# A two-layer decode kernel: one q weight block kept from its first read, a place made of small buffers, and K loads one head further ahead

## The chip, the cores and the metric

The kernel runs on one core of a Trainium2 chip. A core has a matrix engine (PE, whose weight loads are shown apart as PEld), a vector engine (DVE), a scalar engine (ACT), a general one (POOL) and a sync engine (SP) that here does nothing but issue transfers from HBM; 16 DMA engines carry them. Each engine runs its own instructions in order, and engines wait for each other through semaphores. The metric is the device time of one execution in microseconds (us).

## What is computed

Four residual blocks: attention with a cached window, a gated feed-forward block (GLU), and the same two again with the same weights and the same caches.

```python
x = x + attn(layernorm(x));  x = x + glu(layernorm(x))
x = x + attn(layernorm(x));  x = x + glu(layernorm(x))

def attn(x):                          # x: [4, 1, 512], 32 query heads, 8 KV heads of 128
    q = (x @ wq).reshape(4, 1, 32, 128).transpose(0, 2, 1, 3)
    k, v = k_cache[:, :, -2048:], v_cache[:, :, -2048:]     # each repeated for 4 query heads
    p = softmax(q @ k.T * 128 ** -0.5)
    return (p @ v).transpose(0, 2, 1, 3).reshape(4, 1, 4096) @ wo

def glu(x):                           # 512 -> 1792 -> 512
    return (sigmoid(x @ w_gate) * (x @ w_up)) @ w_down
```

The batch is 4. K and V of one KV head and all four batches are 2 MB each in bf16, the q and output weights 4 MB each, the three GLU weights 1.8 MB each.

## The kernel before

**Memory.** `arena` has 50 slots of 128 x 2048 bf16 (512 KB). Two neighbouring slots are a tile (1 MB). 32 slots hold K of all eight heads: K is read once, and the second layer uses it again. The other 18 slots are nine tiles that a pool hands out in turn: for q weights, output weights (four tiles, kept for the second layer), V, and the GLU weights. A tile goes back to the pool when its last user has been recorded; `done` counts users, `fill` takes the next load from the list when the pool, or a named place, has room. Beside the arena lie some 25 small buffers, among them `prow` (the probabilities of one head), `ebuf` (probabilities after transposition, in two halves, one for even and one for odd heads), `qbd` and `qh` (q as the score matmuls need it) and `mxt`.

**Half places.** At the change of layers, weights come in blocks of half a tile. Each block has a home in `homes`: a half of a tile that an earlier load left. Tile names are those of their first occupants: `Y` and `Z` (the two V blocks of head 7), `GA` (the first V block of head 6) and `GB` (a tile taken for nothing but its two halves, after the first layer's loads). A home is written as a pair, such as `(GB, 1)` for the second half. V of head 7 must stay for the second layer; parts of it are stashed in PSUM by transposes on DVE (L578, L600) and brought back (L593, L606), which frees halves of `Y` and `Z`.

**Order of transfers.** SP issues the list in order (L398), each transfer waiting for its place alone: q weights (4 tiles), K of heads 0 and 1, then per head h: K of head h + 2, the output weights of two heads (for h = 0, 2 and 4), V of head h in two blocks. Then the last output weights (a block and two halves), gate and up weights (4 blocks of 448 KB each), down weights (3 blocks of 4 columns of 512 and one of 2), the q weights again in eight blocks of 512 KB, V of heads 6 to 0 as far as it was not kept, and the GLU weights again. A load that waits for its place holds all behind it.

**Order of compute.** Every operation is recorded with what it reads and writes; a list scheduler with estimated durations and due times fixes each engine's order at build time, and semaphore waits are derived from it. For one head of the first layer: four DVE transposes of K (L854), a mask (L872) and the scores (L883) on PE, the maximum on DVE (L896 to L908), the exponential on ACT (L911), a permutation on PE, ACT and DVE (L924 to L931), 32 matmuls with V (L973) for each of the two V blocks, normalisation on DVE (L981, L996) and the output weights (L1162). The second layer's q comes in two halves of four blocks each (`q_mms`, L795): the half `i = 1` first, which serves heads 7 to 4, then `i = 0`. In the second layer two places that last held q blocks become work buffers (`wide_buffers`); each head's scores free two K tiles, which V then uses.

Of the kernel before, what the change touches and what calls it, by code (L numbers as in the profile page):

```python
# [6 lines left out]
F32 = mybir.dt.float32  # L7
BF16 = mybir.dt.bfloat16
# [270 lines left out]
def build(nc, A_x, A_k, A_v, A_wq, A_wo, B_wg, B_wu, B_wd, out, cfg=None):  # L279
# [28 lines left out]
    FCC = 2 * SLOT // D  # L308

# [12 lines left out]
    with es:  # L322
# [9 lines left out]
        ones_f = sb("ones_f", [128, 32], F32)  # L332
        perm = sb("perm", [128, 128], BF16)
        sel_f = sb("sel_f", [128, NR], F32)
        sel_b = sb("sel_b", [128, NR], BF16)
        s3 = sb("s3", [128, 2 * 3], BF16)
        sres = sb("sres", [128, 2], F32)
        sel_r = sb("sel_r", [128, 2 * REP], F32)
        maskr = sb("maskr", [128, 32], F32)
        mxt = sb("mxt", [128, 2 * 32], F32)  # L340
        nmax = sb("nmax", [128, 6], F32)
        msk_s = sb("msk_s", [128, 32], BF16)
        msk_m = sb("msk_m", [128, 2], BF16)
        psm = sb("psm", [128, 2], F32)
# [4 lines left out]
        maskp = sb("maskp", [128, REP], F32)  # L349
        msks = sb("msks", [128, 22], F32)  # L350
# [4 lines left out]
        lnr = sb("lnr", [128, 2 * NB], F32)  # L355
        lnd = sb("lnd", [128, NB], F32)
        lnv = sb("lnv", [128, NB], F32)
        inv_d = sb("inv_d", [128, 1], F32)
# [4 lines left out]
        ident = ebuf[:, 0:64].bitcast(BF16)  # L363
        ps = es.enter_context(nc.psum_tensor("ps", [128, 8, 512], F32))
# [14 lines left out]

        def slot_ap(s):  # L380
            return arena[:, s * SLOT:(s + 1) * SLOT]

# [39 lines left out]
        GB = ("pair",)  # L422
        base = {}
# [10 lines left out]
        def take_load():  # L434
            take_k()
            assert can_take()
            name, emit = loads.pop(0)
            if name in homes:
                hfree.difference_update(home(name))
                s = home(name)[0]  # L440
            else:
                s = pool.alloc()
            where[name] = s
            if name in (Y, Z, GA, GB):
                base[name] = s
            if name == GB:
                hfree.update((s, s + 1))
            emit(s)
# [38 lines left out]
        def load_half(name, src, rate, size, where_):  # L487
            left[name] = 1
            homes[name] = [where_]
            on_free[name] = lambda s: hfree.add(s)  # L490

            def emit(s):
                dma(str(name), slot_ap(s)[:, 0:size], src, w=[("slot", s)], rate=rate)
            loads.append((name, emit))
# [59 lines left out]
        def load_glu(k):  # L554
            for nm, src in (("wg", wg_d), ("wu", wu_d)):
                if k == 0:
                    for c in range(NC):
                        load_half((nm, c, k), src[:, c, :], "bw_3k", F,
                                  (((GB, 0), (GB, 1), (GA, 0), (Y, 0)), ((Y, 1), (Z, 0), (GB, 0), (GB, 1)))[nm == "wu"][c])
                    continue  # L560
                for cc in range(NC // 2):
                    load((nm, cc, k), 2, "bw_3k", (2 * F, src[:, 2 * cc:2 * cc + 2, :], False))
            for (a, b) in bounds_of(k):
# [45 lines left out]
        def load_v(h, bp, k, n_use):  # L609
            name = ("V", h, bp, k)  # L610
            tiles = {(HKV - 2, 0): ((Y, 0),), (HKV - 3, 1): ((Y, 1), (GB, 0))}.get((h, bp)) if k else None
            if tiles is not None:
                halves[h, bp] = []
                for n, tile in enumerate(tiles):
                    half = ("Vh", n, h, bp, k)
                    load_half(half, pair_d(A_v, h, bp)[:, :, n * SLOT:(n + 1) * SLOT], "bw_4k", SLOT, tile)
                    halves[h, bp].append((half, 0))
                if len(tiles) == 1:
                    halves[h, bp].append((KEPT, 0))
                return  # L620
            load(name, n_use, "bw_8k", (2 * SLOT, pair_d(A_v, h, bp), True))
# [9 lines left out]

        P.op("gpsimd", "ones", 200.0, lambda g: g.memset(ones_f[:], 1.0), w=[("ones_f",)])
        P.op("gpsimd", "ident_b", 300.0,
# [9 lines left out]
        for jh in range(2):  # L643
            for bp in range(2):
                for i in range(2):
                    z0 = 16 * jh + 8 * bp + REP * i
                    P.op("gpsimd", "perm%d_%d_%d" % (jh, bp, i), 200.0,
                         lambda g, jh=jh, bp=bp, i=i, z0=z0: g.affine_select(
                             perm[:, :].rearrange("p (a z) -> p a z", a=4)[:, :, z0:z0 + REP],
                             ones_f[:, 0:NR].rearrange("p (a r) -> p a r", a=4),  # L650
                             [[-REP, 4], [-1, REP]], ALU.is_equal, 0.0,
                             base=-(64 * jh + 32 * bp + 16 * i), channel_multiplier=1),
                         r=[("ones_f",), ("perm",)], w=[("perm", jh, bp, i)])
# [5 lines left out]
             r=[("ones_f",)], w=[("msk_s",)])  # L659
# [4 lines left out]
             r=[("ones_f",)], w=[("msk_m",)])  # L664
        P.op("vector", "sel_f", 200.0,
             lambda v: v.tensor_reduce(sel_f[:, :], perm[:, :].rearrange("p (g x) -> p x g", x=NR), AXX, ALU.add),
             r=perms, w=[("sel_f",)])
        P.op("gpsimd", "sel_b", 200.0, lambda g: g.tensor_copy(sel_b[:, :], sel_f[:, :]),
             r=[("sel_f",)], w=[("sel_b",)])
        P.op("vector", "sel_r", 100.0,  # L670
             lambda v: v.tensor_reduce(sel_r[:, :], sel_f[:, :].rearrange("p (g y) -> p y g", g=2), AXX, ALU.add),
             r=[("sel_f",)], w=[("sel_r",)])
# [111 lines left out]
        def q_mms(k, i, qb, cs):  # L784
            for c in cs:
                name, o = wq_part(k, c, i)
                s = need(name)

                src = slot_ap(s) if k else tile_ap(s)
                rd = tok(s)[:1] if k else tok(s)  # L790

                def e_q(pe, c=c, src=src, o=o):
                    last = None
                    for hh in range(4):
                        last = pe.matmul(ps[32 * hh:32 * hh + NB, qb, :], xn[:, c * NB:(c + 1) * NB],  # L795
                                         src[:, o + hh * 512:o + (hh + 1) * 512],
                                         start=(c == 0), stop=(c == NC - 1))
# [373 lines left out]
        def attn_first():  # L1171
# [8 lines left out]
            for h in range(HKV):  # L1180
# [124 lines left out]
        def glu(k, b0, b1, add=None, last=False):  # L1305
# [6 lines left out]
            NH = NFC * nb  # L1312
            NF = F // 4
            half = D // 2

            def x_rows():
# [3 lines left out]
                     lambda g: g.affine_select(idf, ones_f[:, 0:1].broadcast_to([128, 128]), [[1, 128]], ALU.is_equal, 0.0,  # L1320
                                               base=0, channel_multiplier=-1),
                     r=[("ones_f",)], w=[("prow",)])
# [11 lines left out]
            for n, nm in enumerate(("wg", "wu")):  # L1334
                for c in range(NC):
# [3 lines left out]
                    def e_g(pe, c=c, s=s, n=n):  # L1339
                        last = None  # L1340
                        for g in range(4):
# [4 lines left out]
                         r=[("slot", s), ("xn",)], w=[("gu", n)], banks=(gub[n],))  # L1346
# [8 lines left out]
                if n == 0:  # L1355
                    P.op("vector", "gs%d" % k, c_dve(NH),
                         lambda v: v.tensor_tensor(egv, tv, lnr[:, 0:nb].unsqueeze(1).broadcast_to([128, NFC, nb]), ALU.mult),
                         r=[("e", 0), ("e", 1), ("lnr", 0)], w=[("eg",), ("q", 0)])
# [11 lines left out]
                 r=[("e", 0), ("e", 1), ("eg",), ("q", 0)], w=[("hT",)])  # L1370
            if last:
                x_rows()
                for (a, b) in bounds_of(k):
# [3 lines left out]
                    def e_d(pe, a=a, b=b, s=s):  # L1377
                        last_ = None
                        src = tile_ap(s)
                        for fc in range(a, b):  # L1380
# [7 lines left out]
                         r=tok(s) + [("hT",)], w=[("orow",)], banks=(PBS[0],))  # L1388
# [10 lines left out]
            for (a, b) in bounds_of(k):  # L1399
# [3 lines left out]
                def e_d(pe, a=a, b=b, s=s):  # L1403
                    last = None
                    src = slot_ap(s)
                    for fc in range(a, b):
# [7 lines left out]
                     r=tok(s)[:1] + [("hT",)], w=[("cb",)], banks=(CB,))  # L1414
# [24 lines left out]
        loads.append((GB, lambda s: None))  # L1439
# [97 lines left out]
```

## Time and profile before

| | |
|---|---|
| Median of 3 runs | 178.61 us (178.56 to 178.66) |
| Span of the profiled execution, first to last instruction | 177.0 us |
| PE / DVE / ACT / POOL busy | 102.3 / 104.6 / 32.7 / 21.6 us |
| Share of the chain of waits: DMA / DVE / PE | 38% / 32% / 18% |
| HBM read | 70.26 MB |
| Time from issue to landing, V blocks / second q blocks (median) | 22.4 / 6.2 us |

The profile is of one execution. In the views, a line such as L398 is that of the kernel's source, `x8` counts instructions or transfers, and an arrow `out<-in` names what is written and read. In the chain of waits each row gives a start, a length and what was at work; a DMA row runs from its issue to its landing. In a window row, each engine's busy time stands with its instruction count in brackets; then come the granted PE clock, the DMA engines' busy share and their rate.

SP's timeline shows the queue: K and V are issued far ahead, and at the change of layers each block a few microseconds ahead.

```profile
62.12 24.83 SPq L398 DMA_DIRECT2D arena<-in_A_v_cache_dram  x6
95.72 1.30 SPq L398 DMA_DIRECT2D arena<-in_A_wo_dram  x3
97.06 4.95 SPq L398 DMA_DIRECT2D arena<-in_B_w_gate_dram  x4
...
113.03 9.84 SPq L398 DMA_DIRECT2D arena<-in_A_wq_dram  x8
123.83 17.84 SPq L398 DMA_DIRECT2D arena<-in_A_v_cache_dram  x14
```

The columns are start, length from the first to the last of the group's issues, queue, line, transfer and count.

### The profile page before, as it was taken

How to read it: one execution, taken by the hardware profiler on the slowest of the kernel's cores; microseconds unless marked ns; L12 is line 12 of the kernel's file. 1: busy time of each engine (PE TensorE's matmuls, PEld its weight loads, DVE VectorE, ACT ScalarE, POOL GpSimd, SP SyncE). 2: the span in 40 equal slices, each digit the busy share in tenths (PEclk: the TensorE clock that was granted, in tenths of full speed). 3: DMA queues.
4: the chain of work that ended last, by engine and by line, in shares of the span. 5: the costliest groups of instructions: out<-in, count | busy, mean ns of one | idle time of the engine just before them, and what ended most of it. 6: DMA issues, size and time to landing. Idle time of an engine off the chain costs nothing.

```text
span 177.0 us, 3893 instructions
## 1 busy us (share of the span) xinstructions
PE 102.3 (58%) x1641; PEld 55.0 (31%) x1653; DVE 104.6 (59%) x256; ACT 32.7 (18%) x87; POOL 21.6 (12%) x88
## 2 busy tenths in 40 slices
PE   0536236382842634607418866456886999776663
PEld 0203112241431431603404852052323444435322
DVE  7307997838477375594383772304299999742351
ACT  2002031312030210300301101000043365430011
POOL 6100010101010100100100100000011454342000
PEclk9999999999999999999999999999999999975555
DMA  6999999999999999999999999999999999999980
GB/s 179 418 429 428 420 422 416 416 420 426 411 414 429 415 422 418 415 420 426 411 420 428 400 403 403 409 401 387 404 429 409 420 418 422 413 417 405 413 351 28
DMA packets 12882, 70.52 MB, mean 398 GB/s; under 512 B 1336, under 2 KB 1344, under 8 KB 6720
## 3 DMA queue, kind: packets, MB, share of 16 engines
q1 hardware_dynamic: 12856, 70.26, 97.4%
q8 instruction: 13, 0.21, 0.5%
q14 instruction: 5, 0.04, 0.1%
q10 hardware_dynamic: 8, 0.00, 0.0%
HBM read 70.26 MB, written 0.00 MB: 397 GB/s over the span
## 4 chain that ended last, share of the span: by engine, by line
DMA 38%; DVE 32%; PE 18%; issue 4%; SPq 4%; ACT 2%; DVEq 0%; ACTq 0%
DMA arena<-in_B_w_down_dram 15%; DMA arena<-in_A_v_cache_dram 15%; DVE arena L854 11%; PE ps L883 7%; DVE nmax L896 5%; DMA arena<-in_B_w_gate_dram 4%; DMA arena<-in_A_wq_dram 4%; SPq L398 4%; PE ps L973 3%; PE ps L872 2%; DVE nmax L900 2%; DVE mxt L904 2%; DVE ebuf L931 2%; PE ps L1162 2%; DVE arena L1064 2%
## 5 line engine op out<-in xcount | busy, mean ns | idle before, releaser
L854 DVE STREAM_TRANSPOSE arena<-arena 128x1024 f32<-128x1024 f32 x32 | 37.0, 1202 | 0.0
L883 PE MATMUL ps<-arena,qbd 128*32 128x512 bf16 x256 | 25.6, 537 | 0.0
L896 DVE TENSOR_REDUCE nmax<-ps 128x1 f32<-128x512 f32 x16 | 10.8, 675 | 19.4 <-PE ps L883 19.3
L973 PE MATMUL ps<-ebuf,arena 128*128 128x8 bf16 x576 | 17.7, 168 | 7.5 <-DMA arena<-in_A_v_cache_dram 4.4
L872 PE MATMUL ps<-msk_m,msk_s 128*32 128x512 bf16 x64 | 8.6, 526 | 23.1 <-DVE arena L854 21.8
L973 PEld LDWEIGHTS ps<-ebuf,arena 128*128 128x128 bf16 x576 | 16.8, 104 | 9.5 <-DMA arena<-in_A_v_cache_dram 5.5
L911 ACT ACTIVATE prow<-ps,nmax 128x512 bf16<-128x512 f32 x16 | 11.0, 687 | 35.1 <-DVE nmax L908 29.5
L847 ACT CAST qbd<-ps 128x256 bf16<-128x256 f32 x16 | 5.9, 370 | 45.0 <-PE ps L883 35.1
L940 POOL CAST s<-psm 128x1 bf16<-128x1 f32 x9 | 1.7, 187 | 84.0 <-ACT prow L911 84.0
L883 PEld LDWEIGHTS ps<-arena,qbd 128*32 128x32 bf16 x256 | 8.4, 121 | 10.4 <-issue 7.7
L795 PE MATMUL ps<-arena,xn 128*4 128x512 bf16 x64 | 8.5, 572 | 4.9 <-DMA arena<-in_A_wq_dram 4.4
L926 ACT CAST prow<-ps 128x512 bf16<-128x512 f32 x16 | 9.4, 585 | 9.9 <-PE ps L973 2.1
L1342 PE MATMUL ps<-arena,xn 128*4 128x448 bf16 x64 | 7.7, 547 | 4.2 <-DMA arena<-in_B_w_up_dram 1.9
L931 DVE STREAM_TRANSPOSE ebuf<-prow 128x256 f32<-128x256 f32 x16 | 7.0, 435 | 3.8 <-ACT prow L926 3.7
L872 PEld LDWEIGHTS ps<-msk_m,msk_s 128*32 128x32 bf16 x64 | 1.7, 98 | 24.1 <-DVE arena L854 22.7
L773 ACT ACTIVATE lnv<-ps 128x4 f32<-128x4 f32 x4 | 0.7, 173 | 41.0 <-PE ps L769 41.0
L1055 PE MATMUL ps<-arena,ebuf 128*32 128x512 bf16 x112 | 7.9, 405 | 0.2 <-DVE nmax L908 0.2
L842 PE MATMUL ps<-qh,eyew 32*128 32x64 bf16 x64 | 5.6, 217 | 3.7 <-ACT qbd L847 2.4
L807 DVE STREAM_TRANSPOSE ebuf<-ps 128x512 f32<-128x512 f32 x3 | 2.1, 717 | 9.4 <-PE ps L795 9.3
L1351 DVE STREAM_TRANSPOSE ebuf<-ps 128x448 f32<-128x448 f32 x4 | 2.6, 650 | 7.1 <-PE ps L1342 7.1
L1162 PE MATMUL ps<-onp,arena 128*128 128x16 bf16 x144 | 5.3, 175 | 2.5 <-DVE onp L996 2.2
L981 DVE TENSOR_TENSOR onb<-ps,rinv 128x16 bf16<-128x16 f32 x9 | 1.7, 185 | 8.3 <-PE ps L973 8.1
(112 smaller groups left out, 132.2 us busy)
## 6 DMA issues: line engine op xcount, KB each, us to landing
arena<-in_A_v_cache_dram SPq DMA_DIRECT2D x27, 1024.0 KB, 22.4
arena<-in_A_k_cache_dram SPq DMA_DIRECT2D x16, 1024.0 KB, 25.1
arena<-in_A_wq_dram SPq DMA_DIRECT2D x4, 1024.0 KB, 8.0
arena<-in_A_wq_dram SPq DMA_DIRECT2D x8, 512.0 KB, 6.2
arena<-in_A_wo_dram SPq DMA_DIRECT2D x3, 1024.0 KB, 26.2
arena<-in_B_w_down_dram SPq DMA_DIRECT2D x4, 512.0 KB, 6.4
arena<-in_B_w_gate_dram SPq DMA_DIRECT2D x4, 448.0 KB, 8.3
arena<-in_B_w_up_dram SPq DMA_DIRECT2D x4, 448.0 KB, 6.2
```

The lines of the kernel that those rows point to most:

```text
L795: last = pe.matmul(ps[32 * hh:32 * hh + NB, qb, :], xn[:, c * NB:(c + 1) * NB], src[:, o + hh * 512:o + (hh + 1) * 512], start=(c == 0), s ...
L854: P.op("vector", "T%d_%d" % (h, t), c_dve(1024), lambda v, v32=v32: v.transpose(v32, v32), r=[("slot", 4 * h + t)], w=[("slot", 4 * h + t)])
L872: last = pe.matmul(ps[32 * gi:32 * gi + 32, bank, :], msk_s[:, :], msk_m[:, :].unsqueeze(1).broadcast_to([128, 256, 2]), start=True, stop= ...
L883: last = pe.matmul(ps[32 * gi:32 * gi + 32, bank, :], qbd[:, q0:q0 + 32], kt[:, cp // 2, cp % 2, jh * NJ:(jh + 1) * NJ, :], start=False, s ...
L896: lambda v: v.tensor_reduce(nmax[:, k2:k2 + 1], ps[:, bank, :], AXX, ALU.max),
L911: lambda a: a.activation(prow[:, :].rearrange("p (m x t) -> p m x t", x=32, t=2), ps[:, bank, :].rearrange("p (m t x) -> p m x t", x=32, t ...
L926: P.op("scalar", "pc" + tag, c_act(512), lambda a: a.copy(prow[:, :], ps[:, pb, :]), r=[("ppb", pb)], w=[("prow",)], banks=(pb,))
L931: P.op("vector", "pt" + tag, c_dve(256), lambda v: v.transpose(et, prow[:, :].bitcast(F32)), r=[("prow",)], w=[("e", k2)])
L973: last = pe.matmul(ps[:, ob, bp * 8:bp * 8 + 8], src[:, j * 128:(j + 1) * 128], ev[:, j % 2, j % 16 // 2, x0:x0 + 8], start=(j == 0), stop ...
L1055: last = pe.matmul(ps[32 * g:32 * g + 32, ob, :], ew[:, g, mq, t], src.rearrange("p (m t d) -> p t m d", t=2, d=128)[:, t], start=(n == 0) ...
L1162: last = pe.matmul(ps[:, WB, c * NR:(c + 1) * NR], tile_ap(s)[:, o + r_ * D + c * 128:o + r_ * D + (c + 1) * 128], ov[:, r_ * NR:(r_ + 1) ...
L1342: last = pe.matmul(ps[32 * g:32 * g + NB, gub[n], 0:NF], xn[:, c * NB:(c + 1) * NB], slot_ap(s)[:, g * NF:(g + 1) * NF], start=(c == 0), s ...
```

## The change

It has four parts.

1. `WQ` names the tile of the first q weight block, `("wq", 0, 0)`. It is no longer given back after the first layer's q: its second half keeps the data, which is the second layer's block `("wq", 0, 1, 1)` (`keep_wq`), and its first half becomes a half place. The second layer's q weights are seven transfers in place of eight.
2. The pair `GB` is gone. Eight tiles rotate in the first layer in place of nine.
3. `prow`, `qbd`, `qh`, `mxt` and `ebuf` become parts of one buffer `side`; its first 2048 columns are a slot of their own, `SP`, used between the layers for a gate block, a down block and a q block. A transfer into it carries the tokens of all buffers in it (`stok`), and it is given free at the first layer's head 6. The other small buffers are packed into `small`; `hT` moves onto `rinv`, the GLU's `eg` from `qbd` to `onp`, and the constant of ones onto `ebuf`, with one extra memset for `one`. The down blocks become 3, 4, 4 and 3 columns.
4. `AHEAD = 3`: K of heads 0 to 2 come before the first V, and K of head h + 3 before V of head h.

```diff
+    AHEAD = 3
...
-        prow = sb("prow", [128, 512], BF16)
-        ebuf = sb("ebuf", [128, 512], F32)
-        qbd = sb("qbd", [128, 2 * NB * 4 * NR], BF16)
-        qh = sb("qh", [128, 2 * 64], BF16)
+        side = sb("side", [128, 1536 + 1024], BF16)
+        prow, qbd, qh = side[:, 0:512], side[:, 512:512 + 2 * NB * 4 * NR], side[:, 1024:1024 + 2 * 64]
+        mxt = side[:, 1152:1152 + 4 * 32].bitcast(F32)
+        ebuf = side[:, 1536:1536 + 1024].bitcast(F32)
+        small = sb("small", [128, 60], F32)
...
-        hT = sb("hT", [128, NFC * NB], BF16)
+        hT = rinv[:, 0:NFC * NB // 2].bitcast(BF16)
-        eg = qbd[:, 0:2 * NFC * NB].bitcast(F32)
+        eg = onp[:, 0:2 * NFC * NB].bitcast(F32)
...
+        side_toks = [("prow",)] + [(n, i) for n in ("q", "qh", "mk") for i in range(2)]
+        def stok(s, n=SLOT):
+            return [("slot", s)] + (side_toks if s == SIDE else []) + ([("e", 0)] if s == SIDE and n > 1536 else [])
...
-        GB = ("pair",)
-        base = {}
+        WQ = ("wq", 0, 0)
+        SP = ("side",)
+        base = {SP: SIDE}
...
-            return [(a, min(NFC, a + 4)) for a in range(0, NFC, 4)] if k < NG else bounds[:-1] + [(bounds[-1][0], NFC - 2), (NFC - 2, NFC)]
+            return [(0, 3), (3, 7), (7, 11), (11, NFC)] if k < NG else bounds[:-1] + [(bounds[-1][0], NFC - 2), (NFC - 2, NFC)]
...
-                    for c in range(NC):
+                    for c in range(i, NC):
                         load_half(("wq", c, k, i), wq_d[:, c, i * SLOT:(i + 1) * SLOT], "bw_4k", SLOT,
-                                  (((Y, 1), (GB, 0), (GB, 1), (GA, 0)), ((GB, 0), (GB, 1), (GA, 0), (Y, 0)))[i][c])
+                                  (((Y, 0), (Y, 1), (WQ, 1), (WQ, 0)), (None, (WQ, 0), (GA, 0), (SP, 0)))[i][c])
...
-                                  (((GB, 0), (GB, 1), (GA, 0), (Y, 0)), ((Y, 1), (Z, 0), (GB, 0), (GB, 1)))[nm == "wu"][c])
+                                  (((WQ, 0), (GA, 0), (SP, 0), (Y, 0)), ((Y, 1), (Z, 0), (WQ, 0), (GA, 0)))[nm == "wu"][c])
...
-                              ((GA, 0), (Y, 0), (Y, 1), (Z, 0))[a // 4])
+                              ((SP, 0), (Y, 0), (Y, 1), (Z, 0))[n])
...
-            tiles = {(HKV - 2, 0): ((Y, 0),), (HKV - 3, 1): ((Y, 1), (GB, 0))}.get((h, bp)) if k else None
+            tiles = {(HKV - 2, 0): ((GA, 0),), (HKV - 3, 1): ((Y, 0), (Y, 1))}.get((h, bp)) if k else None
...
+        def keep_wq(s):
+            hfree.add(s)
+            name = ("wq", 0, 1, 1)
+            where[name] = s + 1
+            left[name] = 1
+            on_free[name] = lambda s: hfree.add(s)
+        on_free[WQ] = keep_wq
...
+                if h == HKV - 2:
+                    give(SIDE)
...
-        for h in range(2):
+        for h in range(AHEAD):
             loads.append((("K", h), lambda _, h=h: load_k(h)))
         for h in range(HKV):
-            if h + 2 < HKV:
-                loads.append((("K", h + 2), lambda _, h=h + 2: load_k(h)))
+            if h + AHEAD < HKV:
+                loads.append((("K", h + AHEAD), lambda _, h=h + AHEAD: load_k(h)))
...
-        loads.append((GB, lambda s: None))
```

More of the change, by code (lines that the diff above doesn't have):

```diff
@@ L326, in build @@
         arena = sb("arena", [128, NS * SLOT], BF16)
-        prow = sb("prow", [128, 512], BF16)
-        ebuf = sb("ebuf", [128, 512], F32)
-        qbd = sb("qbd", [128, 2 * NB * 4 * NR], BF16)
-        qh = sb("qh", [128, 2 * 64], BF16)
+        side = sb("side", [128, 1536 + 1024], BF16)
[3 more added lines that the diff above has]
+        small = sb("small", [128, 60], F32)
+        one, inv_d, sres, psm, nmax = (small[:, a:b] for a, b in ((0, 1), (1, 2), (2, 4), (4, 6), (6, 12)))
+        s3, msk_m = small[:, 12:15].bitcast(BF16), small[:, 15:16].bitcast(BF16)
+        maskp, lnr, lnd, lnv, msks = (small[:, a:b] for a, b in ((16, 20), (20, 28), (28, 32), (32, 36), (36, 58)))
         eyew = sb("eyew", [128, 224], BF16)
-        ones_f = sb("ones_f", [128, 32], F32)
         perm = sb("perm", [128, 128], BF16)
-        sel_f = sb("sel_f", [128, NR], F32)
         sel_b = sb("sel_b", [128, NR], BF16)
-        s3 = sb("s3", [128, 2 * 3], BF16)
-        sres = sb("sres", [128, 2], F32)
         sel_r = sb("sel_r", [128, 2 * REP], F32)
         maskr = sb("maskr", [128, 32], F32)
-        mxt = sb("mxt", [128, 2 * 32], F32)
-        nmax = sb("nmax", [128, 6], F32)
         msk_s = sb("msk_s", [128, 32], BF16)
-        msk_m = sb("msk_m", [128, 2], BF16)
-        psm = sb("psm", [128, 2], F32)
         rinv = sb("rinv", [128, 2 * NR], F32)
@@ L354, in build @@
         xT = sb("xT", [128, 2 * NX], F32)
[L355 to L358, printed above, removed]
         xn = sb("xn", [128, NX], BF16)
-        hT = sb("hT", [128, NFC * NB], BF16)
+        hT = rinv[:, 0:NFC * NB // 2].bitcast(BF16)
         x_nat = prow[0:NB, 0:D]
-        eg = qbd[:, 0:2 * NFC * NB].bitcast(F32)
+        eg = onp[:, 0:2 * NFC * NB].bitcast(F32)
         ident = ebuf[:, 0:64].bitcast(BF16)
+        sel_f = ebuf[:, 64:64 + NR]
+        ones_f = ebuf[:, 96:128]
         ps = es.enter_context(nc.psum_tensor("ps", [128, 8, 512], F32))
@@ L377, in build @@
         CB = 7
+        SIDE = NS
+        side_toks = [("prow",)] + [(n, i) for n in ("q", "qh", "mk") for i in range(2)]
         def slot_ap(s):
+            if s == SIDE:
+                return side[:, 0:SLOT]
             return arena[:, s * SLOT:(s + 1) * SLOT]
+        def stok(s, n=SLOT):
+            return [("slot", s)] + (side_toks if s == SIDE else []) + ([("e", 0)] if s == SIDE and n > 1536 else [])
         def tile_ap(s):
@@ L443, in take_load @@
             where[name] = s
-            if name in (Y, Z, GA, GB):
+            if name in (Y, Z, GA, WQ):
                 base[name] = s
-            if name == GB:
-                hfree.update((s, s + 1))
             emit(s)
@@ L492, in emit @@
             def emit(s):
-                dma(str(name), slot_ap(s)[:, 0:size], src, w=[("slot", s)], rate=rate)
+                dma(str(name), slot_ap(s)[:, 0:size], src, w=stok(s, size), rate=rate)
             loads.append((name, emit))
@@ L562, in load_glu @@
                     load((nm, cc, k), 2, "bw_3k", (2 * F, src[:, 2 * cc:2 * cc + 2, :], False))
-            for (a, b) in bounds_of(k):
+            for n, (a, b) in enumerate(bounds_of(k)):
                 if k == 0:
                     load_half(("wd", a, k), wd_d[:, a:b, :].rearrange("p k n -> p (k n)"), "bw_4k", (b - a) * D,
-                              ((GA, 0), (Y, 0), (Y, 1), (Z, 0))[a // 4])
+                              ((SP, 0), (Y, 0), (Y, 1), (Z, 0))[n])
                 else:
@@ L630, in build @@
         on_free[GA] = keep_half
+        def keep_wq(s):
[5 more added lines that the diff above has]
+        on_free[WQ] = keep_wq
         P.op("gpsimd", "ones", 200.0, lambda g: g.memset(ones_f[:], 1.0), w=[("ones_f",)])
+        P.op("gpsimd", "one", 100.0, lambda g: g.memset(one[:], 1.0), w=[("one",)])
         P.op("gpsimd", "ident_b", 300.0,
@@ L789, in q_mms @@
                 src = slot_ap(s) if k else tile_ap(s)
-                rd = tok(s)[:1] if k else tok(s)
+                rd = stok(s) if k else tok(s)
                 def e_q(pe, c=c, src=src, o=o):
@@ L1312, in glu @@
             NH = NFC * nb
+            hts = [("rinv", 0), ("rinv", 1)]
             NF = F // 4
@@ L1319, in x_rows @@
                 P.op("gpsimd", "idf", 500.0,
-                     lambda g: g.affine_select(idf, ones_f[:, 0:1].broadcast_to([128, 128]), [[1, 128]], ALU.is_equal, 0.0,
+                     lambda g: g.affine_select(idf, one[:, 0:1].broadcast_to([128, 128]), [[1, 128]], ALU.is_equal, 0.0,
                                                base=0, channel_multiplier=-1),
-                     r=[("ones_f",)], w=[("prow",)])
+                     r=[("one",)], w=[("prow",)])
                 def e_x(pe):
@@ L1387, in glu @@
                     P.op("tensor", "gd%d_%d" % (k, a), (b - a) * 200.0, e_d,
-                         r=tok(s) + [("hT",)], w=[("orow",)], banks=(PBS[0],))
+                         r=tok(s) + [("hT",)] + hts, w=[("orow",)], banks=(PBS[0],))
                     done(name)
@@ L1413, in glu @@
                 P.op("tensor", "gd%d_%d" % (k, a), (b - a) * NC * tm["pe_pair"], e_d,
[L1414 removed]
+                     r=stok(s, (b - a) * D) + [("hT",)] + hts, w=[("cb",)], banks=(CB,))
                 done(name)
```

20 lines of the change are left out of this document (9 added, 11 removed).

## The prediction

> **What bounds the kernel now.** I read the page first, then the chain of waits in order of time, then two-microsecond windows, then SP's timeline, and last the answers of line L398 for one issue at a time.
>
> ```profile
> span 177.0 us, 3893 instructions
> DMA  6999999999999999999999999999999999999980
> q1 hardware_dynamic: 12856, 70.26, 97.4%
> arena<-in_A_wq_dram SPq DMA_DIRECT2D x8, 512.0 KB, 6.2
> ```
>
> The 16 DMA engines are busy in every slice after the first and carry 70.26 MB. The last line is the second layer's q weight, eight blocks of 512 KB; the change drops one of them.
>
> ```profile
> 99.00 2.65 PE ps L973 x96
> 101.68 7.34 DMA arena<-in_B_w_gate_dram
> ...
> 118.07 6.36 DMA arena<-in_A_wq_dram
> 124.47 0.60 PE ps L795 x4
> ...
> 152.67 20.90 DMA arena<-in_B_w_down_dram
> 173.57 0.04 issue
> 173.62 0.60 PE ps L1383 x12
> 174.21 0.03 issue
> 174.24 0.41 PE ps L1383 x8
> ```
>
> The chain runs through compute from 34.6 to 101.7, which would suggest that compute sets the end. But it closes on a transfer issued at 152.67 that lands 20.90 us later: it spent that time in a full queue. So the end is the queue's, and compute matters only where it releases a place too late for the next transfer.
>
> ```profile
> 114.00:116.00 2.00, 0.71 (x20) 0.51 (x16) 0.87 (x2) 0.00 (x0) 0.00 (x0) 1.00 1.02 401
> 120.00:122.00 2.00, 1.73 (x14) 0.69 (x11) 1.67 (x4) 0.16 (x1) 0.00 (x0) 1.00 1.02 412
> 172.00:174.00 2.00, 1.41 (x48) 1.05 (x48) 0.00 (x0) 0.00 (x0) 0.00 (x0) 0.50 0.28 102
> ```
>
> The last two numbers are DMA share and GB/s. Even at the change of layers the share stays at 1. The last row says that a few engines finish late, and a landing needs them all.
>
> **The saving.** One block is 128 x 2048 bf16 = 0.524 MB. At the 401 to 412 GB/s of its windows that is 1.27 to 1.31 us; by the trace's landing marks the eight blocks land 1.23 to 1.29 apart. I take 1.27. The down projection's blocks become 3, 4, 4 and 3 columns of 512 in place of 4, 4, 4 and 2: the same bytes, nothing.
>
> **What the changed order costs.** I call lead the time from an issue to the landing of the transfer ahead of it. The need is bounded by rows. The kernel's first DMA is issued at 0.79 and lands after 5.0 us with nothing ahead; 1 MB blocks land 2.48 apart, so 5.03 - 2.48 = 2.55 us suffice. From above, the smallest leads of the trace without a late landing are 3.86 (issue at 120.56, ahead landing 124.42) and 3.87 (128.16; 132.03). So the need lies between 2.55 and 3.86; I take 2.55, a direct reading.
>
> *First layer, one tile less.* The first tile of q weights now stays, so the nine rotating tiles become eight and each release serves the load one place earlier. V of head 7, second half (V7b) now waits for the first half of head 5's PV (PV5a). If compute stood still that is 95.72, where SP issues the output weight today after that release; V7a lands at 99.42, a lead of 3.70, enough by the value taken.
>
> But K one head ahead moves compute. Two more K blocks stand before V0, so V0 to V4 land 2 x 2.48 = 4.97 us later, V0b at 42.0 for 37.0. K7 lands at 79.5 for 86.96 (V4 and the output weight no longer precede it). From V5 on, the bytes before each V are equal again: V5a lands at 89.45 as now. In the built order S7, the last head's scores, stands before PV4 and not before PV5, and 16 K transposes (12 before) precede the first normalisation, so the wait for V0 is filled. Head by head with trace durations (four L854 4.49; four L872 and 16 L883 2.35; 32 L973 1.03): transposes of K7 end at 82.8 (its second block, 79.5, plus the rest), S7 at 85.2, PV4b waits for its landing at 87.0 and ends 88.1, PV5a waits until 89.45 and ends 90.5. The lead for V7b is then 99.42 - 90.5 = 8.9; the smallest of its neighbours is 8.1. Cost nothing; the cover is arrival of V, and if PV5a ends past 96.9 each further microsecond costs one.
>
> *Change of layers.* Six half places rotate before and after; the side place takes the part of the pair's second half. Its first DMA waits for readers of the probability row and of ebuf's first half: PV6b, near 98 (landing 96.9 plus its matmuls), with a lead over 8, and V7a's and V7b's stash, which free the next places, hang on landings that do not move. Five q blocks again cover the wait for the second layer's normalisation; the sixth needs the kept block's matmuls done, at about 120.65 (12 closing matmuls for 8 add 0.14), a lead of 3.77.
>
> Its second half of q, and then scores, come earlier: the four first blocks need three landings, so the last is in at 121.86 for 123.15. PE is then the limit: two blocks, the variance matmul, two blocks end at 123.05 for 123.79; S2.0 ends at about 127.3 for 128.14. That release issues the next V block: the DMA position is 1.27 ahead, compute 0.87, so this lead falls from 3.87 to 3.46. By 2.55 nothing is lost; by 3.86, 0.40. Queued behind it on SP are the other V loads, each freed by the next scores; after two heads the leads grow, as they do today.
>
> *The end.* Last landing 174.20 - 1.27 = 172.93, and the 2.83 us after it (closing matmuls, copies, output DMA) stay. Compute before it: even at today's times the last up-projection group, no longer waiting until 169.87, starts at 169.45; everything is 0.42 earlier, and the closing matmuls end at 173.42 against 173.38 by DMA. With 0.87 gained in the scores it is hidden. Copying small buffers into shared tensors adds one memset on POOL before q is in: hidden by q's landing at 13.2.
>
> Sum: 177.0 - 1.27 = 175.8 for the profiled execution, bounds 175.7 (by 1.31) and 176.2 (0.40 lost). The median of the runs, 178.61, lies 1.6 above the span; the same difference gives 177.34.
>
> **The rivals.** *(B) A bubble after S2.0:* need nearer 3.86: 0.40 given back, 177.74. For it: bursts of DMA read slower around 123 (windows 122 to 124 show 350 GB/s). Against: landings there are still 1.3 apart.
>
> *(C) Nothing comes out,* 178.6: the landing that ends the run is of the most delayed engines (28% share above), and code loads ("instruction" packets on the page, each about a microsecond on one engine) decide which. One more on a late engine costs 1.3 and eats the gain; one fewer would give 176.0. PE's instruction count is unchanged, so neither is likely. Should a transfer come back elsewhere, the change would not do what it says; the built order has seven q blocks, so no.
>
> *(D) Slower: V's 4.97 us ride through the first layer.* The chain has no DMA piece from 34.6 to 101.7; if all of it moves, PV5a ends at 95.72 + 4.97 = 100.69, V7b lands 5.03 later at 105.72 for 101.88, and 3.84 - 1.27 = 2.57 are lost: 181.2. It loses from PV5a at 96.9 and is slower than before from 98.1. Against it is the head-by-head count, 90.5.
>
> *(E) The matrix clock stays low in the second layer:* 16 L1055 take 1.05 there and 1.65 in the throttled end, 16 L883 1.08 to 1.12 and in the first layer 1.73; eight heads of 0.62 and six of 0.60 are 8.6, less 0.85 of slack: 185.1. The granted clock is 1.00 for both kinds of L883, so that row does not tell.
> The Trainium skill ("TensorE: Matmul & The Clock Gate", Part 1: The HAM clock gate) says that an idle window of about 3.4 us brings half clock and a busy one full clock. Here the durations agree with it (L872 four-fold 0.62 after 4.40 us idle, 0.40 after 0.44), the clock row does not. By that rule longer waits for V in the first layer would leave it as slow as it is, and the second layer warms as before; by the row nothing changes.
>
> **How the numbers follow.** My forecast (full saving) 0.70, own range 177.1 to 177.6. B 0.12; C with no gain 0.05, with a double gain 0.02; D 0.09; E 0.02. Faster than 0.2% (what a measurement of this kernel can tell): 0.70 + 0.12 + 0.02 = 0.84; within 0.05; slower 0.11. The range 176.9 to 178.7 takes A, B and C's no gain, and leaves D, E and the double gain, 0.13.
>
> **What would show it.** 69.7 MB read; seven q blocks of 512 KB; DMA share 1 throughout; SP's issue of V7b before 93; last transfers landing near 172.9; the first V block after the scores issued near 127.3 with landing less than 6.5 us later; L1383 still ended by DMA. Wrong if a window between 95 and 140 shows a share clearly under 1 with landings over 2.6 us apart for 1 MB, if PV5a ends after 97, or if L1383 no longer waits for a DMA.

## The result, and the profile after

The changed kernel takes 177.49 us (median of 6 runs, 177.15 to 177.77), the kernel before 178.63 beside it (6 runs): a ratio of 0.993, 95% interval 0.9907 to 0.9952. So it is faster, by 1.14 us; 177.34 was forecast. The profiled execution took 177.70, with a span of 175.9. Of the runs of the experiments below, one (180.12, V7b after PV6a) was disturbed and is left out.

Four lines of the changed kernel's page, the same as were shown of the page before: the span, the DMA engines' busy tenths by slice, the queue that carries the loads (packets, MB, share of 16 engines), and the second layer's q blocks.

```profile
span 175.9 us, 3909 instructions
DMA  5999999999999999999999999999999999999990
q1 hardware_dynamic: 12712, 69.74, 97.4%
arena<-in_A_wq_dram SPq DMA_DIRECT2D x6, 512.0 KB, 6.3
```

The queue carries 0.52 MB less, the size of one block, at the same share of its time (97.4%), and the span is 1.1 us shorter. Six q blocks go to the arena, and a seventh to the place made of small buffers (its row names `side` and is not among these).

The chain of waits, in order of time (start, length, what was at work):

```profile
63.00 0.96 PE ps L982 x32
63.98 22.92 DMA arena<-in_A_v_cache_dram
86.94 1.03 PE ps L982 x32
87.99 11.30 DMA arena<-in_A_v_cache_dram
99.32 1.33 DVE ps L578 x2
...
155.70 16.72 DMA arena<-in_B_w_down_dram
172.47 0.60 PE ps L1395 x15
173.10 0.41 PE ps L1395 x7
```

L982 is the matmuls with V, L973 before. From 63 to 99 the chain now consists of V transfers, where before it was compute: in the first layer compute stands and waits for V. One group of the page (busy time and mean of one in ns, then idle time before it and what ended it) gives the sum of that waiting:

```profile
L982 PE MATMUL ps<-side,arena 128*128 128x8 bf16 x576 | 18.2, 168 | 13.4 <-DMA arena<-in_A_v_cache_dram 13.4
```

The same group of the kernel before:

```profile
L973 PE MATMUL ps<-ebuf,arena 128*128 128x8 bf16 x576 | 17.7, 168 | 7.5 <-DMA arena<-in_A_v_cache_dram 4.4
```

That is 13.4 us of waiting for V, where the kernel before waited 7.5 in all and 4.4 of it for V. This extra 9 us costs nothing, because the chain closes as before: on the last down blocks, issued long before, with the closing matmuls (L1395, L1383 before) waiting for them. The last transfer lands at 173.06 by its landing mark, for 174.20.

SP's timeline (start, length from first to last issue of the group, line, transfer, count):

```profile
86.02 4.98 SPq L399 DMA_DIRECT2D arena<-in_A_v_cache_dram  x3
92.94 1.30 SPq L399 DMA_DIRECT2D arena<-in_A_wo_dram  x3
```

The last of the three V issues is V7b, at 90.47. V7a, ahead of it, lands at 99.30, so its lead (the time from an issue to the landing of the transfer ahead) is 8.8 us. The output weight after it is issued at 92.94, for 95.72 before.

### The profile page after: what moved, and what is told of

Read it like the earlier page. It is cut to its first block, busy times and chain, and to the rows that moved or that the text cites. A ratio compares the mean times of both kernels' runs of the same rounds, so it can differ in the third digit from the quotient of the medians.

```text
span 175.9 us, 3909 instructions
## 1 busy us (share of the span) xinstructions
PE 106.1 (60%) x1653; PEld 54.2 (31%) x1653; DVE 104.2 (59%) x256; ACT 32.7 (19%) x87; POOL 21.7 (12%) x89
## 3 DMA queue, kind: packets, MB, share of 16 engines
q1 hardware_dynamic: 12712, 69.74, 97.4%
## 4 chain that ended last, share of the span: by engine, by line
DMA 47%; DVE 33%; PE 15%; issue 2%; SPq 1%; POOL 1%; ACT 0%; DVEq 0%
DMA arena<-in_A_v_cache_dram 19%; DMA arena<-in_B_w_down_dram 13%; DVE arena L863 12%; DMA arena<-in_A_wq_dram 10%; PE ps L892 7%; DMA arena<-in_B_w_gate_dram 5%; DVE small L905 5%; PE ps L881 2%; DVE arena L1073 2%; DVE small L909 2%; DVE side L913 2%; DVE side L940 2%; DVE arena L1078 1%; DVE arena L593 1%; DVE small L917 1%
## 5 line engine op out<-in xcount | busy, mean ns | idle before, releaser
L982 PE MATMUL ps<-side,arena 128*128 128x8 bf16 x576 | 18.2, 168 | 13.4 <-DMA arena<-in_A_v_cache_dram 13.4
L892 PE MATMUL ps<-arena,side 128*32 128x512 bf16 x256 | 25.2, 527 | 0.0
L982 PEld LDWEIGHTS ps<-side,arena 128*128 128x128 bf16 x576 | 16.8, 104 | 19.7 <-DMA arena<-in_A_v_cache_dram 17.2
L905 DVE TENSOR_REDUCE small<-ps 128x1 f32<-128x512 f32 x16 | 10.8, 676 | 17.6 <-PE ps L892 17.5
L920 ACT ACTIVATE side<-ps,small 128x512 bf16<-128x512 f32 x16 | 11.0, 687 | 36.7 <-PE ps L1000 18.4
L881 PE MATMUL ps<-small,msk_s 128*32 128x512 bf16 x64 | 8.6, 526 | 14.3 <-DVE arena L863 13.7
L892 PEld LDWEIGHTS ps<-arena,side 128*32 128x32 bf16 x256 | 8.3, 120 | 10.2 <-issue 7.5
L935 ACT CAST side<-ps 128x512 bf16<-128x512 f32 x16 | 9.4, 585 | 10.8 <-PE ps L933 10.8
L933 PE MATMUL ps<-side,perm 128*128 128x512 bf16 x16 | 8.1, 507 | 5.0 <-ACT side L920 4.9
L1064 PE MATMUL ps<-arena,side 128*32 128x512 bf16 x112 | 8.2, 416 | 0.2 <-DVE small L917 0.2
L940 DVE STREAM_TRANSPOSE side<-side 128x256 f32<-128x256 f32 x16 | 6.9, 433 | 2.2 <-ACT side L935 2.0
```

The costliest lines, as they stand in the source:

```text
L881: last = pe.matmul(ps[32 * gi:32 * gi + 32, bank, :], msk_s[:, :], msk_m[:, :].unsqueeze(1).broadcast_to([128, 256, 2]), start=True, stop= ...
L892: last = pe.matmul(ps[32 * gi:32 * gi + 32, bank, :], qbd[:, q0:q0 + 32], kt[:, cp // 2, cp % 2, jh * NJ:(jh + 1) * NJ, :], start=False, s ...
L905: lambda v: v.tensor_reduce(nmax[:, k2:k2 + 1], ps[:, bank, :], AXX, ALU.max),
L920: lambda a: a.activation(prow[:, :].rearrange("p (m x t) -> p m x t", x=32, t=2), ps[:, bank, :].rearrange("p (m t x) -> p m x t", x=32, t ...
L933: lambda pe: pe.matmul(ps[:, pb, :], perm[:, :], prow[:, :], start=True, stop=True),
L935: P.op("scalar", "pc" + tag, c_act(512), lambda a: a.copy(prow[:, :], ps[:, pb, :]), r=[("ppb", pb)], w=[("prow",)], banks=(pb,))
```

## The experiments

Each is compared with the kernel before on the same chip, whose median there is 178.64 to 178.72. The ratios are taken against it; losses in microseconds are taken against the changed kernel's 177.49, which was measured beside a kernel before of 178.63. Three questions: is it the bytes that were saved; what is K one head further ahead for; and how long a lead does the queue need?

### The kept block read again

```diff
-            while loads and loads[0][0][0] == "K":
+            while loads and loads[0][0][0] in ("K", "again"):
...
+                loads.append((("again",), lambda _: dma("again", slot_ap(base[WQ] + 1), wq_d[:, 0, SLOT:2 * SLOT],
+                                                       w=[("slot", base[WQ] + 1)])))
```

> The changed kernel with one more transfer: the kept q block is read again into the place where it already lies, as the first of the second layer's q blocks; places, tiles and orders of the change stay. 'Bytes': +1.27 us on 177.5, 178.7 to 178.8, last landing near 174.3. 'Order': 177.5.

Measured: 178.60 (178.39 to 178.82), ratio 0.9988 (0.9976 to 1.0001). Everything else of the change is in it, and its HBM read is again 70.26 MB. The end of its chain:

```profile
152.28 20.92 DMA arena<-in_B_w_down_dram
173.25 0.60 PE ps L1397 x15
173.88 0.41 PE ps L1397 x7
```

The closing matmuls stand 0.78 later than in the changed kernel (this execution, at 178.39, was the fastest of its runs). On the medians 1.11 of the 1.14 us are gone with the bytes put back; by the ratios 0.0058 of 0.0070, and the 0.0012 that is left is not told from nothing. The gain is the block not read.

### K three heads ahead in the kernel before

```diff
-        for h in range(2):
+        for h in range(3):
...
-            if h + 2 < HKV:
-                loads.append((("K", h + 2), lambda _, h=h + 2: load_k(h)))
+            if h + 3 < HKV:
+                loads.append((("K", h + 3), lambda _, h=h + 3: load_k(h)))
```

> The kernel before with K three heads ahead and nothing else changed: eight q blocks, nine rotating tiles. 'Bytes': 178.6, same as before, though PV5a ends near 90.5 and the chain of waits in the first layer becomes one of DMA waits for V. 'Order': some of the 1.1 us of gain appears, 177.5 to 178.2.

Measured: 178.64 (178.46 to 179.73), ratio 0.9999 (0.9975 to 1.0023). The output weights after head 7's V are issued from 90.4 on instead of 95.7, and nothing comes of it. The order of K and V is worth nothing by itself.

### The changed kernel with K two heads ahead

```diff
-    AHEAD = 3
+    AHEAD = 2
```

> The changed kernel with K two heads ahead again; the kept block, the side place and eight rotating tiles stay. Theory 'bytes' (time follows the bytes in a queue that never empties; a lead of 2.55 us is enough): V7b is issued after a PV5a near 95.7, a lead of about 3.7, no landing is late: 177.5, as the changed kernel. Rival 'order' (K further ahead is what pays): back to 178.6. Rival 'carry' read the other way (without K ahead the release is too late): over 178.6, with 1 MB landings near 102 more than 2.6 apart.

Measured: 178.39 (177.58 to 179.60, 12 runs), ratio 0.9977 (0.9956 to 0.9998). V7b is issued at 95.58 and V7a lands at 99.16: a lead of 3.58, near the 3.70 that the prediction had worked out for compute standing still, and called enough. It is not: 0.9 of the 1.14 us are lost on the median. Two windows of its profiled execution, one of its fastest at 177.70, and then the first of them in the changed kernel (stretch, length, busy time of PE, PEld, DVE, ACT, POOL, granted clock, DMA share, GB/s):

```profile
97.00:98.00 1.00, 0.30 (x4) 0.34 (x5) 0.09 (x1) 0.30 (x3) 0.60 (x4) 1.00 0.82 270
98.00:99.00 1.00, 0.81 (x30) 0.82 (x31) 0.68 (x3) 0.40 (x1) 0.15 (x1) 1.00 0.96 385
...
97.00:98.00 1.00, 0.88 (x32) 0.79 (x30) 0.00 (x0) 0.00 (x0) 0.00 (x0) 1.00 1.05 442
```

The queue is short of work at 97, two microseconds before V7a lands, and moves 270 GB/s; the changed kernel has a share of 1.05 and 442 GB/s in that window. (Share and rate count a packet where it starts, so a share can pass 1.) So the fourth part of the change is what makes the first part pay.

### V7b held back: leads from 6.5 down to 1.4

Four kernels equal the changed one but for one more dependency of V7b's load: on the landing of V6b, or on one of the PV matmuls just before.

```diff
+        held = [o for o in P.ops if o.name == str(("V", HKV - 1, 1, 0))]
+        late = [o for o in P.ops if o.name == "PV0.6_6_0"]
+        held[0].deps.add(late[0])
```

(`PV0.5_5_1` and `PV0.6_6_1` in the other two; for the landing, the load of V6b in the place of `late`.) On the first of them:

> The changed kernel in which the issue of V7b waits for the landing of V6b (96.8) too, so that its lead is about 2.45 us by the trace's landing of V7a at 99.3. Need 2.55: at most 0.1 lost, 177.5 to 177.7. Need 3.86: 1.4 lost, 178.9, with V7b landing 3.9 after V7a in place of 2.5.

On the others:

> The changed kernel with one dependency more: the load of V7b also waits for the second half of head 5's PV (PV5b). V5b lands at 91.8 and its matmuls take 1.03, so the issue moves from 90.5 to about 92.9, and the lead from 8.8 to 6.4. By the forecast's need of 2.55 and by a need of 4.5 to 5 (what the runs with leads of 3.58 and 2.43 suggest) nothing is lost: 177.5. Only if any delay of this issue costs, whatever the lead, would it be slower: by its 2.4, near 180.

> The same, V7b waiting for the first half of head 6's PV (PV6a): V6a lands at 94.3, PV6a ends near 95.4, lead 3.9. By the forecast's need of 2.55, and also by its upper bound of 3.86, nothing is lost: 177.5. By a need of 4.5 to 5, 0.6 to 1.1 is lost: 178.1 to 178.6.

> The same, V7b waiting for the second half of head 6's PV (PV6b): V6b lands at 96.8, PV6b ends near 97.9, lead 1.4. By a need of 2.55, 1.15 is lost: 178.65. By a need of 4.5 to 5, 3.1 to 3.6 is lost: 180.6 to 181.1.

The leads are from each profiled execution: V7a's landing mark less V7b's issue. The loss is the median less 177.49. The last column is from the same execution as the lead: the time from V7a's landing to that of the first layer's last down block, some 118 us into the run.

| Kernel | V7b issued | Lead | Median (range) | Ratio to before (95%) | Loss | V7a to last down block |
|---|---|---|---|---|---|---|
| Changed kernel | 90.47 | 8.8 | 177.49 (177.15 to 177.77) | 0.993 (0.9907 to 0.9952) | | 18.77 |
| After PV5b | 92.75 | 6.5 | 177.78 (177.22 to 178.30) | 0.994 (0.9916 to 0.9963) | 0.3 | 18.63 |
| After PV6a | 95.40 | 3.8 | 178.2 (177.35 to 179.00, 11 runs) | 0.996 (0.994 to 0.998) | 0.7 | 19.58 |
| K two ahead | 95.58 | 3.6 | 178.39 (177.58 to 179.60) | 0.9977 (0.9956 to 0.9998) | 0.9 | 19.05 |
| After landing of V6b | 96.76 | 2.4 | 180.18 (179.20 to 180.76) | 1.0073 (1.0049 to 1.0097) | 2.7 | 19.99 |
| After PV6b | 97.88 | 1.4 | 181.24 (180.98 to 181.27) | 1.0128 (1.011 to 1.0147) | 3.75 | 20.90 |

The last two rows differ by 1.07 in lead and 1.06 in time: below some lead each microsecond costs about one. Lead and loss add up to 5.1 in both, and to 4.5 at 3.8 and at 3.6, so by the time of the whole run the need is about 4.5 to 5. The loss at a lead of 6.5 is not told from none (the intervals overlap almost wholly); that at 3.8 by itself is not either (0.994 to 0.9952 is in both), and it is the row beside it, at 3.6, whose interval lies outside. The best run at a lead of 3.8 took 177.35, within the changed kernel's range, and others 178.5 and more.

The last column says how much of that arises where the lead was cut. The profiled executions with leads of 6.5 and more (the kernel before and the other experiments among them) take 18.58 to 18.77 for this stretch, in the middle 18.63. Above that, 0.95 is lost at a lead of 3.8, 0.4 at 3.6, 1.4 at 2.4 and 2.3 at 1.4. Lead and this loss add up to 3.6 and 3.8 at the two shortest leads, 4.0 at 3.6 and 4.8 at 3.8. These are single executions; that at 3.8, at 179.00, is the slowest of its runs, and that at 3.6 one of the fastest. So at the place itself the need is 3.6 to 4.8, and at the two shortest leads about a microsecond of the loss comes from elsewhere or from other executions. Why was not tried. After 118 us the second layer's V landings slip in every execution of the table, by 0.7 to 2.6 us in all (against 2.48 us for each 1 MB block and 1.27 for each half of one), so such differences need no short lead at V7b.

The shortest lead shows what happens. Windows of its profiled execution, cut to where the last two columns (DMA share, GB/s) change:

```profile
95.40:96.40 1.00, 0.00 (x0) 0.00 (x0) 0.00 (x0) 0.00 (x0) 0.00 (x0) 1.00 1.01 410
96.40:96.80 0.40, 0.00 (x0) 0.00 (x0) 0.00 (x0) 0.00 (x0) 0.00 (x0) 1.00 0.81 307
96.80:97.60 0.80, 0.76 (x28) 0.77 (x29) 0.00 (x0) 0.00 (x0) 0.00 (x0) 1.00 0.54 225
97.60:98.60 1.00, 0.25 (x10) 0.16 (x7) 0.00 (x0) 0.00 (x0) 0.00 (x0) 1.00 0.35 147
98.60:99.20 0.60, 0.00 (x0) 0.00 (x0) 0.00 (x0) 0.00 (x0) 0.00 (x0) 1.00 0.01 0
99.20:100.20 1.00, 0.92 (x32) 0.92 (x32) 0.94 (x2) 0.00 (x0) 0.00 (x0) 1.00 0.96 328
100.20:101.20 1.00, 0.36 (x8) 0.20 (x5) 0.86 (x3) 0.00 (x0) 0.00 (x0) 1.00 0.92 377
```

V7a is the last transfer in the queue here. Its engines run out one after another: the first between 96.4 and 96.8, the last near 98.6, and the landing comes at 99.24. V7b is issued at 97.88 and its first bytes move at 99.2, 1.3 us later (in the kernel below, 1.3 us too). So some engine is idle unless the next issue comes 2.6 + 1.3 = 3.9 us before the landing (99.24 less 96.6, and 99.2 less 97.88). And after the gap the rate is lower for its share: 328 GB/s at 0.96 and 377 at 0.92, for 442 at 1.05 in the changed kernel's window above. The landing of V6b as the release (lead 2.4) shows the same:

```profile
96.00:97.00 1.00, 0.21 (x8) 0.21 (x8) 0.00 (x0) 0.00 (x0) 0.00 (x0) 0.50 0.82 328
97.00:98.00 1.00, 0.81 (x31) 0.72 (x27) 0.00 (x0) 0.00 (x0) 0.00 (x0) 0.50 0.43 180
98.00:99.00 1.00, 0.00 (x0) 0.00 (x0) 0.00 (x0) 0.00 (x0) 0.00 (x0) 0.50 1.07 320
99.00:100.00 1.00, 0.76 (x28) 0.76 (x29) 0.78 (x2) 0.00 (x0) 0.00 (x0) 0.50 0.93 377
```

At 98 the share is 1.07 and only 320 GB/s go through, so a byte takes 1.4 times as long as at 442 and 1.05. The 3.9 for no engine to idle lies inside the 3.6 to 4.8 found at the place; the slow restart adds to what a gap costs. What slows it was not tried.

The Trainium skill ("DMA: Bandwidth & Descriptors", Why a DMA increments its semaphore by 16 and not by 1) says that the up to 16 engines of a transfer finish independently, and that it has landed when all of them count. The windows agree, with two microseconds between the first engine and the last. The Trainium skill ("DMA: Bandwidth & Descriptors", Anatomy of one DMA — SWDGE (gpsimd) path) gives about 2.0 us of fixed cost for one DMA issued by the general engine instead of SP. A lead of 2.4, longer than that, lost 2.7 us here, so that figure is no measure of how early to issue into a full queue.

### The changed kernel with K four heads ahead

```diff
-    AHEAD = 3
+    AHEAD = 4
```

> The changed kernel with K four heads ahead instead of three: V0 to V3 land another 2.48 us later, the last K blocks earlier, and from V5a on the transfers land as before. If the arrival of V alone times the release of V7b's place (PV5a at its landing 89.4 plus 1.0) the issue stays near 90.5 and the time at 177.5. If the delay of V0 rides through compute into the release (the rival with V's 4.97 us), PV5a ends 2.5 later, near 93, which the lead of 8.8 still covers: 177.5 too, but with the issue at 93. So the time should be the same either way, and the issue of V7b tells them apart.

Measured: 177.45 (177.21 to 177.91), ratio 0.9921 (0.9902 to 0.994): the same as the changed kernel. The answer for V7b's issue in its profile (duration in ns, then first and last start, and the time to landing):

```profile
L399 SPq DMA_DIRECT2D arena<-in_A_v_cache_dram x1: 536/536/536, 90.5 to 90.5; - x1
...
DMA to landing us min/median/max: 11.3/11.3/11.3
```

V0 to V3 land about 5.0 us later (V0b at 46.96 for 41.86), since K of one head is two blocks and not the one that was expected, and V7b is issued at 90.5 all the same. The delay of the first V blocks does not ride through the layer; the arrival of V5a sets the release.

### One more q block not read

```diff
-                dma(str(name), slot_ap(s)[:, 0:size], src, w=stok(s, size), rate=rate)
+                if name != ("wq", 1, 1, 1):
+                    dma(str(name), slot_ap(s)[:, 0:size], src, w=stok(s, size), rate=rate)
```

> The changed kernel with one more second-layer q block not read (the one of columns c = 1, half i = 1): its half place keeps what stood there, so q of heads 7 to 4 is computed with another block in its place, and six q blocks of 512 KB are transferred for seven. All transfers after it stand 1.27 us earlier in the queue, while the releases at the change of layers hang on compute and stay: the block now issued at 120.56 has a lead of about 2.6 for 3.85, and the V block issued after the first scores (126.9) one of about 2.6 for 3.9. By the bytes and a need of 2.55 the time falls by the whole block again, to 177.5 - 1.27 = 176.2 (176.6 if compute becomes the end). By a need of 4.5 to 5 the first of these places alone loses 1.9 to 2.4: nothing is gained, 177.5 to 178.6.

Measured: 178.14 (177.55 to 178.55, 12 runs), ratio 0.9963 (0.9946 to 0.998). HBM read is 69.21 MB, another block less, and the time is 0.65 above the changed kernel's. By the bytes it would have been 176.2, a ratio of 0.986. Two windows of its profiled execution, at 178.22, and then the same two of the changed kernel:

```profile
116.00:118.00 2.00, 0.93 (x29) 0.76 (x27) 0.00 (x0) 0.00 (x0) 0.00 (x0) 1.00 0.94 331
...
124.00:126.00 2.00, 2.00 (x24) 0.66 (x20) 0.00 (x0) 0.22 (x1) 0.00 (x0) 1.00 0.83 264
...
116.00:118.00 2.00, 1.03 (x32) 0.86 (x30) 0.00 (x0) 0.00 (x0) 0.00 (x0) 1.00 1.03 410
...
124.00:126.00 2.00, 2.00 (x24) 0.79 (x25) 0.00 (x0) 0.37 (x1) 0.00 (x0) 1.00 1.01 377
```

The second row follows the issue at 120.31, whose transfer ahead lands at 123.97, a lead of 3.66; the first follows one at 115.52 with a lead of 3.53, behind one at 113.97 with 3.84. Both places are issued only 0.2 to 0.3 earlier than in the changed kernel, since their releases hang on compute, while the queue stands a whole block earlier. The gap at 116 was not expected: it comes two blocks before the place that was named, and by the loss in it the later leads are 3.66 and 4.9, longer than the 2.6 worked out. The queue is out of slack at the change of layers, and what is saved in bytes now is given back in gaps.

## Why the prediction was right, and where it was off

- **The saving.** Right in kind, a little large: 1.27 for the last landing, measured 1.14 (174.20 less 173.06), and 1.11 by reading the block again (1.04 by the ratios). The sum for the span was 175.8, measured 175.9.
- **K further ahead and the first layer.** Right, nearly to the digit: V0b lands at 41.86 (42.0 forecast), K7 at 79.37 (79.5), V5a at 89.37 (89.45), and V7b is issued at 90.47 (90.5). The cover named, the arrival of V, is what the chain shows.
- **The needed lead.** Wrong, in size. 2.55 was taken, bounded above by 3.86. The runs put it at 3.6 to 4.8 at the place itself and at 4.5 to 5 by the whole run: a lead of 2.4 costs 2.7 us, 1.4 of them at the place, where the value taken allows 0.1. The working subtracted 2.48 from the 5.03 of the first transfer alone, which measures from an issue to the end of one transfer. It leaves out that the engines of the transfer ahead run dry up to 2.6 us before its landing. The upper bound came from two issues after which the next landing was not late, and that is the wrong landing to look at. In the execution with a lead of 3.83, V7b lands on time, 2.50 after V7a, and it is the second transfer behind it that is late, 1.17 after the one ahead for 0.68 in the changed kernel; with a lead of 2.43 it is the same one, 1.76 for 0.68. The trace of the kernel before had a late landing too, which the prediction passed over: behind the issue with a lead of 3.87, the one at 130.62 has a lead of 3.92 and lands 3.81 after the one ahead, for 2.48 (it has another possible cause, named below). The forecast held at V7b because the lead there is 8.8, as worked out, which covers either value. At the change of layers, where the leads are 3.8 to 3.9, it was luck that no more than 0.13 was missing. With K two heads ahead, the prediction's "enough by the value taken" would have forecast the full saving, and 0.9 of it was missing.
- **The change of layers.** The sixth q block was issued at 120.56 (120.65 forecast), the first scores end at 126.86 (127.3), and the V block after them is issued at 126.91. Its landing was to come within 6.5 us:

```profile
L399 SPq DMA_DIRECT2D arena<-in_A_v_cache_dram x1: 535/535/535, 126.9 to 126.9; - x1
...
DMA to landing us min/median/max: 7.3/7.3/7.3
```

  It took 7.3 us. That block lands 3.41 after the one ahead and the next 2.82 after that, for 2.48: 1.27 us late in all. The windows there, of the changed kernel and then of the kernel before:

```profile
128.00:130.00 2.00, 1.57 (x25) 0.59 (x21) 1.96 (x5) 0.98 (x3) 0.00 (x0) 1.00 1.15 375
130.00:132.00 2.00, 1.56 (x28) 0.46 (x24) 1.90 (x4) 0.66 (x2) 0.70 (x3) 1.00 0.86 348
...
128.00:130.00 2.00, 2.00 (x24) 0.78 (x24) 1.70 (x6) 0.58 (x2) 0.00 (x0) 1.00 1.03 416
130.00:132.00 2.00, 1.39 (x20) 0.37 (x13) 2.00 (x4) 1.43 (x4) 0.15 (x1) 1.00 1.04 424
```

  So the sign of being wrong that the prediction named, a share clearly under 1 with landings over 2.6 us apart, did show (0.86; 3.41 and 2.82), at the place of rival B and behind a lead of 3.9. Two things can be its cause. One is that lead. The other is an instruction fetch on one of the 16 engines (the page's q8, 13 packets in both kernels), which starts at 133.6. The kernel before has a slip of 1.33 at 138.34, with a fetch at 133.9 and a lead of 3.92. A fetch needs no short lead to go with such a slip: in the first layer, with leads of over 20 us, one at 30.7 in both kernels goes with a landing 1.17 late (1.38 before). But in the changed kernel the rate is down five microseconds ahead of the fetch, which speaks for the lead. The runs do not settle it, nor whether it explains the missing 0.13; that the leads here have nothing to spare, the last experiment shows.
- **The end.** Right: the closing matmuls still wait for the DMA, and the tail after the last landing is 175.9 - 173.06 = 2.84 (2.83 forecast).
- **The rivals.** A bubble after the first scores (B) was priced at 0.40 with the need at its upper bound. The windows above look like one, in one execution, but no loss of that size is seen on the median: the saving fell short by 0.13. That nothing comes out (C) would have needed the bytes to be hidden; reading them again costs 1.11. V's delay riding through the first layer (D) is excluded by V7b's issue at 90.47, and by K four heads ahead, where V0 is 5.0 later again and that issue does not move. The slow matrix clock (E) did not come: the second layer's 112 L1064 (L1055 before) have the same median of 379 ns in both kernels.

Not tried by itself: the third part, the side place with the down blocks of 3, 4, 4 and 3 columns. It was costed at nothing; the kernel that reads the block again contains it, and its ratio of 0.9988 (0.9976 to 1.0001) shows no cost.

## What to carry to other kernels

Where the DMA queue is the bound, a transfer left out is worth its bytes only if the loads behind it can still be issued early enough: compare every issue that waits for a place with the landing of the transfer ahead of it, not with its own landing. Here, with 1 MB transfers, leads of 3.8 us and less opened gaps and one of 6.5 cost nothing that could be told; the engines began to run dry 2.6 us before the landing of the transfer ahead, and the next one's bytes came 1.3 us after its issue. Look for the cost two or three landings further on, and not only at the next one. A change that costs a place should come with one that frees places sooner, as K ahead of V did here; alone that was worth nothing, and without it 0.9 of the 1.14 us was lost.

## What was not expected of the hardware

The sixteen engines of one 1 MB transfer run dry over some 2 us (96.6 to 98.6 with a landing at 99.24), so a queue can be partly idle while its last transfer is still far from landing. After a gap the rate is low for its share for about a microsecond or more: 320 GB/s at a share of 1.07, for 442 at 1.05 without a gap.

The granted clock in the profile's rows is no measure of matmul time here. In the execution with V7b after the landing of V6b it reads 0.50 from 50 to 128 us (it shows in the windows above), in that of the changed kernel 1.00; the score matmuls between 60 and 128 us have a median of 628 ns in both.
